# Reordering the first batch of a retention + phase-MLP kernel by the arrival of its loads

## Chip, cores, metric

One core of one Trainium2 chip. The metric is the device time of one execution in microseconds; lower is better. The four times of the kernel before lie between 171.39 and 173.17 us, 1.0% apart, so differences below that rest on several runs taken in turn with the kernel before.

## The reference, cut to what matters

```python
# retention: B=4, H=8, S=768, D=64
state = gamma * state + k_t (outer) v_t ;  x_t = scale * q_t . state
# then, with x of shape (4, 768, 512):
theta = x @ w_theta
zr, zi = x * cos(theta), x * sin(theta)
u = x + w_tok_r @ zr + w_tok_i @ zi       # mixing over the 768 tokens
out = u + max(u @ w_ch, 0)
```

## The kernel before

A **pair** is two 128-row chunks of one batch (three pairs to a batch). For each pair the kernel loads q, k, v in float32, scales and casts them (`prep`), transposes q and k on TensorE (`flip`), forms masked scores (`ret_A`, `ret_mask`), the product with v (`ret_Y`), the part from the state (`ret_I`), the state's update (`ret_S`), theta and its cosine and sine (`theta`), and z (`zmul`). A **tile** is 128 rows of output: `moe_M` (12 mixing matmuls), `moe_u`, `moe_U` (transpose of u), `moe_O`. `w_tok` transposes one block row of the two token weights. The schedule is by hand: in the traces below each engine takes its instructions in the order of the program, so one that waits holds up everything behind it on its engine (2.93 us of TensorE at one place, below). In profile lines PE is TensorE and PEld its loading of weights, DVE is VectorE, ACT ScalarE, POOL GpSimd.

```python
def prep(n, name, engines):                     # cast / scale of a loaded tensor
    ...
        for two in range(2):                    # q and v: one half on each of two engines
            engines[two].tensor_mul(dst[:, two], src[:, two], ...)
def flip(n, name):
    ps = psum.tile([P, 2, NP, P], BF, name="kq_ps", tag="tr", bufs=2)   # two "tr" banks in all
    ... 8 nc.tensor.transpose ...
    nc.vector.tensor_copy(t, ps)
def moe_O(m):
    o_ps = psum.tile([P, dm], FT, name="o_ps", tag="tr", bufs=2)        # the same two banks
    ...
# ---- cut: the first batch, written out call by call ----
for n in range(nG, B * nG + 1):                 # the loop starts at pair 3 (nG = 3)
    ...
    if nxt:
        prep(n + 1, "q", PP)                    # both halves on GpSimd
        prep(n + 1, "v", PP)
    if n == nG:
        w_cast(4)
        nc.gpsimd.tensor_copy(wch, wdma["ch"])
    ...
        theta(n - 1, 0); x_pe(n - 1); theta(n - 1, 1)
    for name, limit in (("k", K_DMA), ("q", Q_DMA)):
        if nxt and n + 1 < limit:
            flip(n + 1, name)                   # in the middle of the iteration
    ...
    ret_S(n, 0); ...; ret_A(n, 1); ret_mask(n, 1); ret_Y(n, 0); ret_I(n, 0)
    moe_U(done)
    moe_M(first, 2, 4)
    if n in (nG, nG + 1):
        w_tok(n - nG + 4)
    moe_M(first, 4, nT)
    moe_u(first)
    ...
    zmul(n - 1, 0); zmul(n - 1, 1)
    for t in done:
        moe_O(t)
        moe_out(t)
```

## Time and profile before

| | before |
|---|---|
| median time | 172.41 us (171.39 to 173.17, 4 runs) |
| span of the profiled run | 170.4 us |
| TensorE (PE) busy | 158.9 us, 93% |
| granted TensorE clock (share of full speed, profiled run) | 1.00 |
| first PE instruction of iterations 4, 5, 6 (`ret_I`, line L241) | 53.25, 63.02, 72.12 us |

The last row is the ruler: iteration n of the loop starts with the state product of the pair before it, so that line's times cut the run into iterations. From iteration 4 on TensorE has no gap; 98.3 us follow the start of iteration 6. The lines themselves are in the prediction.

### The profile page before, as it was taken

What the parts mean: (1) busy time and instruction counts of PE and PEld (TensorE: products, weight loads), DVE (VectorE), ACT (ScalarE), POOL (GpSimd) and SP (SyncE); (2) the same over time, 40 slices, a digit from 0 to 9 for tenths busy, and PEclk for the clock granted to TensorE, in tenths of its full rate; (3) what the DMA queues carried; (4) which work ended last, traced back from release to release, by engine and by line L of the source; (5) the groups of instructions that cost most, each with busy time, mean ns of one, the idle gap of its engine ahead of it and who ended that gap; (6) DMA issues with size and microseconds to landing.
All of it is one profiled execution on the core that took longest, in us unless ns stands there. A gap on an engine that the chain in (4) does not pass through costs nothing.

```text
span 170.4 us, 4701 instructions
## 1 busy us (share of the span) xinstructions
PE 158.9 (93%) x1979; PEld 88.5 (52%) x1979; DVE 101.3 (59%) x139; ACT 82.7 (49%) x141; POOL 62.4 (37%) x81
## 2 busy tenths in 40 slices
PE   7789898988789999999999999999999999999992
PEld 2255465644455766656465645454455444444470
DVE  2457597885657567797486374671755617334443
ACT  8216686770464959677864744828156170000000
POOL 6284839455699588480908163000000000000000
PEclk9999999999999999999999999999999999999999
DMA  4999999999999999999999995976727161464343
GB/s 129 304 341 313 318 302 351 315 377 272 317 304 340 265 295 344 252 210 252 193 286 294 216 260 118 252 96 142 139 51 197 33 175 41 132 192 115 92 154 123
DMA packets 66789, 37.92 MB, mean 223 GB/s; under 512 B 24144, under 2 KB 61264, under 8 KB 66768
## 3 DMA queue, kind: packets, MB, share of 16 engines
q1 hardware_dynamic: 66624, 37.50, 87.2%
q8 instruction: 15, 0.25, 0.6%
q10 hardware_dynamic: 144, 0.13, 0.2%
q14 instruction: 6, 0.05, 0.1%
HBM read 25.69 MB, written 6.29 MB: 188 GB/s over the span
## 4 chain that ended last, share of the span: by engine, by line
PE 77%; DMA 8%; DVE 3%; POOL 3%; ACT 3%; issue 2%; DVEq 0%; POOLq 0%
PE y_ps L328 32%; PE th_ps L302 12%; PE o_ps L356 12%; DMA pair<-in_q_dram 6%; PE at_ps L204 4%; PE kq_ps L183 3%; PE yT_ps L227 3%; PE yT_ps L241 3%; PE st_ps L258 3%; DMA pair<-in_k_dram 2%; PE y_ps L402 2%; DVE at L211 1%; POOL kqb L175 1%; ACT kqb L169 1%; PE w_ps L382 1%
## 5 line engine op out<-in xcount | busy, mean ns | idle before, releaser
L328 PE MATMUL y_ps<-z,wtr 128*128 128x512 bf16 x138 | 52.4, 380 | 1.3 <-DVE u L335 0.8
L328 PE MATMUL y_ps<-z,wti 128*128 128x512 bf16 x138 | 52.3, 379 | 0.0
L335 DVE TENSOR_TENSOR u<-y_ps,x_sb 128x512 bf16<-128x512 f32 x23 | 15.9, 692 | 30.0 <-PE y_ps L328 29.9
L175 POOL TENSOR_TENSOR kqb<-pair,qscp 128x512 bf16<-128x512 f32 x20 | 21.1, 1073 | 33.1 <-DMA pair<-in_q_dram 27.9
L211 DVE TENSOR_TENSOR at<-at_ps,maskp 128x1024 bf16<-128x1024 f32 x24 | 29.3, 1219 | 3.6 <-PE at_ps L204 3.6
L281 ACT CAST xT<-yT_ps 128x512 bf16<-128x512 f32 x22 | 15.0, 738 | 26.3 <-PE yT_ps L227 26.3
L175 POOL TENSOR_TENSOR kqb<-pair,vscp 128x512 bf16<-128x512 f32 x24 | 25.4, 1079 | 4.1 <-DMA pair<-in_v_dram 4.1
L302 PE MATMUL th_ps<-wth,xT 128*128 128x512 bf16 x96 | 23.5, 379 | 0.1
L363 DVE SCALAR_TENSOR_TENSOR ot<-o_ps,u 128x512 f32<-128x512 f32 x23 | 15.8, 689 | 13.0 <-PE o_ps L356 13.0
L356 PE MATMUL o_ps<-wch,uT 128*128 128x512 bf16 x92 | 22.6, 379 | 0.5 <-POOL wch L582 0.5
L328 PEld LDWEIGHTS <-wti 128*128 128x128 bf16 x138 | 13.5, 98 | 14.7 <-issue 1.7
L328 PEld LDWEIGHTS <-wtr 128*128 128x128 bf16 x138 | 13.5, 98 | 13.8
L305 ACT ACTIVATE cs<-th_ps,halfpi 128x512 bf16<-128x512 f32 x24 | 16.5, 688 | 8.3 <-PE th_ps L302 7.9
L272 ACT CAST stbd<-st_ps 64x256 bf16<-64x256 f32 x40 | 14.7, 368 | 11.9 <-PE st_ps L258 11.3
L186 DVE COPY kqT<-kq_ps 128x1024 bf16<-128x1024 bf16 x17 | 11.5, 687 | 11.1 <-PE kq_ps L183 11.1
L312 DVE TENSOR_TENSOR z<-cs,x_sb 128x1024 bf16<-128x1024 bf16 x24 | 17.4, 763 | 0.4 <-DMA x_sb<-xT 0.4
L306 ACT ACTIVATE cs<-th_ps,zerob 128x512 bf16<-128x512 f32 x24 | 16.5, 687 | 0.0
L356 PEld LDWEIGHTS <-uT 128*128 128x128 bf16 x92 | 8.9, 98 | 11.2 <-issue 0.7
L302 PEld LDWEIGHTS <-xT 128*128 128x128 bf16 x96 | 8.9, 98 | 9.9 <-ACT xT L281 0.6
L169 ACT CAST kqb<-pair 128x1024 bf16<-128x1024 f32 x12 | 12.6, 1048 | 1.6 <-DMA pair<-in_k_dram 1.5
L414 ACT COPY uT<-u_ps 128x256 bf16<-128x256 bf16 x2 | 0.7, 373 | 25.5 <-PE u_ps L413 25.5
L183 PE MATMUL kq_ps<-ident,kqb 128*128 128x128 bf16 x136 | 10.1, 219 | 2.9 <-DVE kqb L175 1.0
(57 smaller groups left out, 161.9 us busy)
## 6 DMA issues: line engine op xcount, KB each, us to landing
pair<-in_k_dram SPq DMA_DIRECT2D x12, 512.0 KB, 6.8
pair<-in_q_dram SPq DMA_DIRECT2D x12, 512.0 KB, 7.6
pair<-in_v_dram SPq DMA_DIRECT2D x12, 512.0 KB, 8.0
out_dram<-ot SPq DMA_DIRECT2D x23, 256.0 KB, 2.4
wtok<-in_moe_w_tok_r_dram SPq DMA_DIRECT2D x6, 384.0 KB, 6.8
wtok<-in_moe_w_tok_i_dram SPq DMA_DIRECT2D x6, 384.0 KB, 6.5
w<-in_moe_w_theta_dram SPq DMA_DIRECT2D x1, 1024.0 KB, 8.0
w<-in_moe_w_ch_dram SPq DMA_DIRECT2D x1, 1024.0 KB, 9.2
```

Source lines behind the costliest of these rows:

```text
L175: engines[two].tensor_mul(dst[:, two], src[:, two], _bcast_last(sc[:, 2 * g + two], D))
L183: nc.tensor.transpose(ps[:, two, j, :], st[n, name][:, two, j * P:(j + 1) * P], ident)
L211: nc.vector.tensor_mul(at.rearrange("p a j t -> p (a j) t"), at_ps.rearrange("p a j t -> p (a j) t"), _bcast_mid(maskp[:, two].rearrange(" ...
L281: copy(st[n, "xT"][:, a].rearrange("e j (i w) -> e j w i", w=2), st[n, "y"][a].rearrange("e j (w i) -> e j w i", w=2))
L302: nc.tensor.matmul(th_ps, st[n, "xT"][:, a, j, :], wth[:, j, :], start=(j == 0), stop=(j == NP - 1))
L305: nc.scalar.activation(cs[:, 0, :], th_ps, AF.Sin, bias=halfpi, scale=1.0)
L306: nc.scalar.activation(cs[:, 1, :], th_ps, AF.Sin, bias=zerob, scale=1.0)
L312: nc.vector.tensor_mul(zs[b][:, c], st[n, "cs", a], _bcast_mid(xs[b][:, c, :], 2))
L328: nc.tensor.matmul(y_ps, wT[r][:, s0, t0 * P:(t0 + 1) * P], zs[b][:, s0, r, :], start=(s0 == 0 and r == 0), stop=(s0 == nT - 1 and r == 1))
L335: nc.vector.tensor_add(u, mo[m]["y"], xs[b][:, t0, :])
L356: nc.tensor.matmul(o_ps, mo[m]["uT"][:, j, :], wch[:, j, :], start=(j == 0), stop=(j == nD - 1))
L363: nc.vector.scalar_tensor_tensor(ot, mo[m]["o"], 0.0, mo[m]["u"], ALU.max, ALU.add)
```

## The change

Its intent: put the first batch in an order that fits the times at which the loads land, so that TensorE works where it waited. On GpSimd: k of pairs 2 and 3 is cast there. In PSUM: tile 1 is summed in the state's bank, so tiles 0 and 1 can be open at once. In the loop's iterations 3 to 5 the flips of the next pair go to the end, where their loads have surely landed, with half of q scaled on VectorE.

```diff
-            if m < (B - 1) * nT - 1:
+            if m == 1:
+                y_ps = psum.tile([P, dm], FT, name="y_ps", tag="st", bufs=1)
+            elif m < (B - 1) * nT - 1:
 ... (the first batch's calls in another order; dummy matmuls 31 -> 27) ...
-    prep(2, "k", K)
+    prep(2, "k", (PL,))
-    prep(3, "k", K)
+    prep(3, "k", (PL,))
 ... in the loop:
-        if nxt:
-            prep(n + 1, "q", PP)
-            prep(n + 1, "v", PP)
+        def preps(engines):
+            prep(n + 1, "q", engines)
+            prep(n + 1, "v", PP)
+            if n in (nG, nG + 1):
+                w_cast(n - nG + 4)
         if n == nG:
-            w_cast(4)
             nc.gpsimd.tensor_copy(wch, wdma["ch"])
+        if nxt and n > nG + 2:
+            preps(PP)
+        if n == nG:                      # after ret_A, ret_mask of pair 3
+            moe_u(1)
+            w_tok(2)
         for name, limit in (("k", K_DMA), ("q", Q_DMA)):
-            if nxt and n + 1 < limit:
+            if nxt and nG + 3 < n + 1 < limit:
                 flip(n + 1, name)
+        if n < nG + 3:
+            prep(n + 1, "k", (AC,))      # behind moe_U
-            if n in (nG, nG + 1):
-                w_tok(n - nG + 4)
             moe_M(first, 4, nT)
             moe_u(first)
+            if n < nG + 3:
+                w_tok(n - nG + 3)
 ... zmul(n - 1, 0), zmul(n - 1, 1) ...
-        for t in done:
+        if n < nG + 3:
+            preps(DP)                    # q: one half VectorE, one GpSimd
+        for i, t in enumerate(done):
+            if n < nG + 3:
+                flip(n + 1, "kq"[i])
+                if len(done) == 1:
+                    flip(n + 1, "q")
             moe_O(t)
             moe_out(t)
```

More of the change, by code (lines that the diff above doesn't have):

```diff
@@ L177, in prep, with flip @@
         st[n, name] = t
-    def flip(n, name):
+    def flip(n, name, copy=nc.vector.tensor_copy):
         ps = psum.tile([P, 2, NP, P], BF, name="kq_ps", tag="tr", bufs=2)
@@ L185, in flip, with flip_out @@
         t = work.tile([P, 2, NP, P], BF, name="kqT", bufs=6)
-        nc.vector.tensor_copy(t, ps)
-        st[n, name + "T"] = t
+        if copy:
+            copy(t, ps)
+        st[n, name + "T"], st[n, name + "_ps"] = t, ps
+    def flip_out(n, name):
+        nc.vector.tensor_copy(st[n, name + "T"], st[n, name + "_ps"])
     def flip_dma(n, name):
@@ L288, in x_dma, with x_pe, x_out @@
             in_=st[n, "xT"].rearrange("p a j t -> p (a j t)"))
-    def x_pe(n, lo=0, hi=2):
+    def x_pe(n, copy=nc.vector.tensor_copy):
         b, g = divmod(n, nG)
-        x_ps = psum.tile([P, hi - lo, NP, P], BF, name="x_ps", tag="tr", bufs=2)
-        for a in range(lo, hi):
+        x_ps = psum.tile([P, 2, NP, P], BF, name="x_ps", tag="tr", bufs=2)
+        for a in range(2):
             for j in range(NP):
-                nc.tensor.transpose(x_ps[:, a - lo, j, :], st[n, "xT"][:, a, j, :], ident)
-        nc.vector.tensor_copy(xs[b][:, 2 * g + lo:2 * g + hi, :],
-                              x_ps.rearrange("p a j e -> p a (j e)"))
+                nc.tensor.transpose(x_ps[:, a, j, :], st[n, "xT"][:, a, j, :], ident)
+        st[n, "x_ps"] = x_ps
+        if copy:
+            x_out(n, copy)
+    def x_out(n, copy):
+        b, g = divmod(n, nG)
+        copy(xs[b][:, 2 * g:2 * g + 2, :],
+             st[n, "x_ps"].rearrange("p a j e -> p a (j e)"))
     def theta(n, a):
@@ L376, in w_cast, with w_flip, w_out @@
             wrow[r, t0] = row
+    def w_flip(r, t0, copy=True):
+        w_ps = psum.tile([P, nT, P], BF, name="w_ps", tag="tr", bufs=2)
+        for s0 in range(nT):
+            nc.tensor.transpose(w_ps[:, s0, :],
+                                wrow[r, t0][:, s0 * P:(s0 + 1) * P], ident)
+        wrow[r, t0, "ps"] = w_ps
+        if copy:
+            w_out(r, t0)
+    def w_out(r, t0):
+        (nc.scalar.copy if r else nc.vector.tensor_copy)(
+            wT[r][:, :, t0 * P:(t0 + 1) * P], wrow[r, t0, "ps"])
     def w_tok(t0):
         for r in range(2):
-            w_ps = psum.tile([P, nT, P], BF, name="w_ps", tag="tr", bufs=2)
-            for s0 in range(nT):
-                nc.tensor.transpose(w_ps[:, s0, :],
-                                    wrow[r, t0][:, s0 * P:(s0 + 1) * P], ident)
-            dst = wT[r][:, :, t0 * P:(t0 + 1) * P]
-            if r:
-                nc.scalar.copy(dst, w_ps)
-            else:
-                nc.vector.tensor_copy(dst, w_ps)
+            w_flip(r, t0)
     def moe_last(m):
@@ L447, in keep_busy @@
             nc.tensor.matmul(warm_ps, warm[:, 0:P], warm, start=True, stop=True)
-    DP, PP, K = (nc.vector, nc.gpsimd), (nc.gpsimd, nc.gpsimd), (nc.scalar,)
+    DV, PL, AC = nc.vector, nc.gpsimd, nc.scalar
+    DP, PP = (DV, PL), (PL, PL)
     keep_busy(12)
-    prep(0, "k", K)
-    flip(0, "k")
-    keep_busy(4)
+    prep(0, "k", (AC,))
+    flip(0, "k", None)
     prep(0, "q", DP)
+    flip_out(0, "k")
+    keep_busy(3)
     flip(0, "q")
@@ L464 @@
     state_out(0, 0)
-    keep_busy(1)
     ret_A(0, 1)
     ret_mask(0, 1)
+    ret_Y(0, 0)
+    keep_busy(1)
     ret_S(0, 1)
+    ret_I(0, 1)
     state_out(0, 1)
-    ret_Y(0, 0)
-    ret_I(0, 1)
-    keep_busy(3)
-    prep(1, "k", K)
-    ret_Y(0, 1)
-    ret_out(0, 0, nc.scalar.copy)
-    ret_out(0, 1, nc.vector.tensor_copy)
-    keep_busy(1)
+    prep(1, "k", (AC,))
+    keep_busy(1)
+    ret_Y(0, 1)
+    ret_out(0, 0, DV.tensor_copy)
+    ret_out(0, 1, DV.tensor_copy)
+    keep_busy(3)
+    prep(1, "q", DP)
+    theta(0, 0)
     flip(1, "k")
-    prep(1, "q", DP)
-    x_pe(0, 0, 1)
-    theta(0, 0)
-    x_pe(0, 1, 2)
     theta(0, 1)
     flip(1, "q")
-    keep_busy(2)
     prep(1, "v", PP)
     w_cast(0)
+    x_pe(0, None)
     ret_A(1, 0)
     ret_mask(1, 0)
-    keep_busy(2)
+    x_out(0, DV.tensor_copy)
+    keep_busy(3)
     ret_S(1, 0)
@@ L494 @@
     ret_mask(1, 1)
-    prep(2, "k", K)
     ret_Y(1, 0)
     ret_I(1, 0)
+    w_flip(0, 0)
     ret_S(1, 1)
@@ L500 @@
     ret_I(1, 1)
-    keep_busy(2)
+    ret_Y(1, 1)
+    ret_out(1, 0, AC.copy)
+    ret_out(1, 1, DV.tensor_copy)
+    w_flip(1, 0)
+    prep(2, "k", (PL,))
     zmul(0, 0)
     zmul(0, 1)
-    ret_Y(1, 1)
-    ret_out(1, 0, nc.scalar.copy)
-    w_tok(0)
-    ret_out(1, 1, nc.scalar.copy)
     prep(2, "q", DP)
+    theta(1, 0)
+    theta(1, 1)
     flip(2, "k")
-    theta(1, 0)
+    moe_M(0, 0, 1)
     flip(2, "q")
@@ L514 @@
     w_cast(2)
-    x_pe(1, 0, 1)
-    moe_M(0, 0, 2)
+    x_pe(1, AC.copy)
+    moe_M(0, 1, 2)
     ret_A(2, 0)
     ret_mask(2, 0)
-    theta(1, 1)
-    x_pe(1, 1, 2)
     ret_S(2, 0)
     state_out(2, 0)
+    zmul(1, 0)
     ret_A(2, 1)
@@ L527 @@
     ret_I(2, 1)
-    zmul(1, 0)
+    moe_M(0, 2, 3)
+    ret_Y(2, 1)
+    ret_out(2, 0, AC.copy)
     zmul(1, 1)
-    ret_Y(2, 1)
-    ret_out(2, 0, nc.scalar.copy)
-    ret_out(2, 1, nc.vector.tensor_copy)
+    ret_out(2, 1, DV.tensor_copy)
     w_tok(1)
+    prep(3, "k", (PL,))
+    prep(3, "q", PP)
+    moe_M(0, 3, 4)
     theta(2, 0)
-    x_pe(2, 0, 1)
     theta(2, 1)
-    x_pe(2, 1, 2)
-    moe_M(0, 2, 4)
+    x_pe(2)
+    flip(3, "k", AC.copy)
     zmul(2, 0)
-    prep(3, "k", K)
-    w_tok(2)
-    moe_M(0, 4, 5)
+    moe_M(1, 0, 4)
     zmul(2, 1)
-    flip(3, "k")
-    moe_M(0, 5, nT)
-    moe_u(0)
-    prep(3, "q", DP)
+    flip(3, "q")
     prep(3, "v", PP)
     w_cast(3)
-    moe_M(1, 0, 4)
-    flip(3, "q")
+    moe_M(0, 4, nT)
+    moe_u(0)
     moe_M(1, 4, nT)
-    moe_u(1)
-    w_tok(3)
-    prep(4, "k", K)
     tiles_of = {nG - 2: [], nG - 1: [0, 1]}
@@ L575 @@
             moe_U_dma(done[1])
-        if nxt:
-            prep(n + 1, "q", PP)
+        def preps(engines):
+            prep(n + 1, "q", engines)
             prep(n + 1, "v", PP)
+            if n in (nG, nG + 1):
+                w_cast(n - nG + 4)
         if n == nG:
-            w_cast(4)
             nc.gpsimd.tensor_copy(wch, wdma["ch"])
-        if n == nG + 1:
-            w_cast(5)
+        if nxt and n > nG + 2:
+            preps(PP)
         if late:
@@ L637 @@
                 moe_M(first, 2, 4)
-            if n in (nG, nG + 1):
-                w_tok(n - nG + 4)
             moe_M(first, 4, nT)
             moe_u(first)
+            if n < nG + 3:
+                w_tok(n - nG + 3)
         elif n in pairs:
             moe_M(mine[1], 0, nT)
-        if n + 2 in pairs:
-            prep(n + 2, "k", K)
+        if n + 2 in pairs and n > nG + 1:
+            prep(n + 2, "k", (AC,))
         if late:
```

## The prediction

> Names: a pair is two 128-row chunks of one batch, three pairs to a batch; pair n is worked on by iteration n of the loop, which starts at pair 3. Flip = transpose on TensorE (PE) into the "tr" banks, two in all, each emptied by a copy on VectorE (DVE) or ScalarE (ACT). prep = cast or scaling of a load. T = the end of the last mixing matmul of an iteration's tile. GpSimd is POOL.
>
> **What bounds the kernel now.** I read the slices first, then the chain in order of time, then the timelines of PE and DVE. The slices:
>
> ```profile
> PE   7789898988789999999999999999999999999992
> DMA  4999999999999999999999995976727161464343
> ```
>
> A slice is 4.26 us. PE is full from slice 13 (51 us) on; before that it has gaps, and 31 dummy matmuls (L447) fill others. So only the first 53 us can be shortened; after that, time is PE work. The chain says what held PE there:
>
> ```profile
> 33.74 10.18 DMA pair<-in_q_dram
> 44.06 1.36 POOL kqb L175 x2
> ...
> 48.05 1.59 POOL wrow L375 x2
> 49.64 1.85 POOL wch L582
> 51.53 1.89 PE o_ps L356 x8
> 53.42 0.22 PE yT_ps L241 x4
> ```
>
> q of pair 4 landed at 44.06; PE, in order, had that flip ahead of pair 3's work, and the output products waited for the cast of w_ch, last in POOL's row. Iteration 4 starts at 53.25. PE's timeline of an undisturbed iteration, and DVE's at the same time:
>
> ```profile
> 53.25 0.39 PE L241 MATMUL yT_ps<-kqT,stbd 128*128 128x128 bf16 x4
> ...
> 57.44 1.06 PE L183 MATMUL kq_ps<-ident,kqb 128*128 128x128 bf16 x16
> ...
> 60.62 0.83 PE L382 MATMUL w_ps<-ident,wrow 128*128 128x128 bf16 x12
> ...
> 62.16 1.03 PE L356 MATMUL o_ps<-wch,uT 128*128 128x512 bf16 x4
> 63.02 0.39 PE L241 MATMUL yT_ps<-kqT,stbd 128*128 128x128 bf16 x4
> ```
>
> ```profile
> 62.36 0.69 DVE L335 TENSOR_TENSOR u<-y_ps,x_sb 128x512 bf16<-128x512 f32 x1 [0.64 <-PE y_ps L328]
> 62.97 1.45 DVE L312 TENSOR_TENSOR z<-cs,x_sb 128x1024 bf16<-128x1024 bf16 x2
> 64.34 0.68 DVE L363 SCALAR_TENSOR_TENSOR ot<-o_ps,u 128x512 f32<-128x512 f32 x1
> ```
>
> Flips and w_tok stand in the middle, with mixing matmuls behind them, so PE runs from T = 62.16 into the output product and the next iteration; DVE's u, two z and ot run behind it and nobody waits. Iterations 4, 5, 6 start at 53.25, 63.02, 72.12.
>
> [...] The trace has 1.89 us for a 2048-wide cast (L459) and 0.82 for 768 (L375), so k's 1024 is an estimate of 1.0 to 1.1 us from these, against 1.05 on ACT. [...] In the trace DVE's q half (128x512) takes 0.77 us at 15.83 and 1.17 to 1.22 at 7.39 and 24.05, with POOL busy on its half.
>
> **The change, part by part.** PE's real work is unchanged (four dummies fewer, 0.9 us, in gaps). I lay the new order of each engine by hand along the loads' arrivals seen in before: the start of the POOL instruction that waited for them. PE costs are distances in the dense stretch: flip 0.45, w_tok 0.67, product of four 512-wide matmuls 0.86, full tile 2.59, attention matmuls 0.22 to 0.35 each group; a consumer on DVE sees PE 0.2 us after its last issue.
>
> *Pair 0, 1.* q's DVE half goes ahead of the copy of k, so the first q flip starts at 8.2, not 8.62, and the scores at 9.6, not 10.03. Both xT casts on DVE and theta ahead of the flip: theta starts at about 14.5 (before 15.72), pair 1's scores at 18.0 (18.90). Then v1 and w0 (cast 19.07 to 20.93, bound by the loads) close the gap.
> *Pair 2.* k2 on POOL about 21.9 to 22.95, q2 not before 23.67. Both thetas of pair 1 now precede pair 2's flips; I get pair 2's scores at 26.9 (27.12), its second yT at 30.5 (30.83), the end of its x transposes at 34.0 (34.25), with 0.86 us of tile 0 more done. Ahead by 1.1.
> *Pair 3 and tiles 0, 1.* w2i's cast waits for a row buffer until w_tok(1), to 32.1; k3 on POOL to 33.2; flip at 34.0. Tile 1 in the state's bank need not wait for u of tile 0 (before: a 0.78 us PE gap at 39.08). q3 flips at 36.2, tiles 0 and 1 end at 38.4, the scores of pair 3 at 38.75. w_tok(2), to 39.4. Tile 2 needs its copy, which stands on DVE behind the mask (1.22) and u of tile 1 (0.61): 41.3, a new gap of 1.9. State, scores, yT, u transposes and the rest of tile 2 bring T to **45.2**; before it is at 51.1, with both flips of pair 4 and w_tok 3 and 4 (2.24 us) already done. Net lead 5.9 - 2.24 = **3.7 us**.
>
> *The end of iterations 3, 4, 5.* The flips of the next pair move behind T, and their q half goes to DVE. In DVE's new order stand u, wtr copy, z, z, q half, copy of k, copy of q, ot (iteration 3 has no z and two ot). In iterations 4 and 5, from T: u begins +0.2, wtr copy +0.8, the two z +1.3 (1.37 together), q half +2.65 to +3.75. The q flip cannot start before +3.8. The copy of k follows to +4.4 and frees the bank that the output product needs: +4.4 to +5.26, next iteration. The PE work behind T is 0.67 + 0.45 + 0.45 + 0.86 = 2.43, so PE idles 5.26 - 2.43 = **2.8 us**; 2.4 if the q half runs at 0.77. In iteration 3, without z: q half +1.3 to +2.4, copy of k +3.0, q flip +3.5, ot, second product to +4.5, against 3.29 of work: **1.2 us**.
>
> *Sum.* Iteration 4 starts at 45.2 + 4.5 = 49.7 (before 53.25). From start to T the dense work is 62.16 - 53.25 - 0.67 - 0.9 = 7.3. Iteration 5: 49.7 + 7.3 + 5.26 = 62.2 (63.02). Iteration 6: + 12.5 = 74.7 (72.12). By then the work done is equal. The balance: -3.7 + 1.2 + 2.8 + 2.8 = +3.1 by the terms, +2.6 by the clock, the difference being PE waits of before (about 0.5, at w_ch) that vanish. With 0.3 off for an uncontended q half in iteration 5, about +2.4: 171.76 + 2.4 = **174.2 us**. From iteration 6 the order is as before and PE was dense.
>
> **Rivals.** *A: the intended gain stays.* Without the DVE chain, iteration 3 would end with the flip of q4 at 45.2 and its second output product at 46.5: 6.7 us ahead, less 0.67 for w_tok(4), so 165.7. For it: the loads are there in time (q5 was used at 51.44 with no DMA wait, q6 landed at 59.22, and my iterations need them at 59.6 and 72). Against it: the flips' new place and DVE's order are fixed in the program, and the u that starts the chain cannot run before T. Even a start at 46.5 loses 5.2 to 5.6 in iterations 4 and 5 and ends near 171.
> *B: the loads become the bound.* q4 to q6 leave their buffers later (q6 at 73 instead of 61), so the load seven pair-loads later (v8, issued at 64.96) goes out near 73, and in SP's queue the transpose of k7 (71.28) comes behind it, at about 75, landing 79 (3.8 us to landing); needed near 83. Slack some 4 us. If it is late, 1 to 2 us more: 176.
> *C: contention.* The pair of z took 2.20 at 72.06 with POOL busy, instead of 1.28 to 1.45. Twice that adds 1.5: 175.7. For it: POOL scales q6 and v6 about when iteration 4's z run.
> *D: my front part is too slow.* 150 instructions laid by hand; an error of 1.5 us either way is likely.
>
> **Range and chances.** Centre 174.2. D gives +-1.5, B and C reach up by 1 to 2 each, A bounds the gain near 171. Eight in ten: 171.8 to 176.6. Slower by over 2% is above 175.2, which C or B alone reaches: 0.29. Faster by over 2% is below 168.3, which needs the stalls not to exist: 0.03. Within 2%: 0.68.
>
> **What would show it.** Right: PE gaps ahead of the q flip and of the output product in iterations 4 and 5, 2.4 to 2.9 us in each, released by DVE (q half; copy of k), with no DMA in that chain; iteration 4 starting at 48.5 to 51, 5 at 61 to 63.5, 6 at 73.5 to 76; the wait for q of pair 4 gone; a PE gap near 40 before tile 2's first matmul, released by the wtr copy; PE full from 76 on. Wrong: PE full from iteration 4 on (A); PE waiting for DMA after 50 us (B); iteration 4 starting before 47.5 or after 51.5 (D).

(The casts at L459 and L375 are GpSimd's.)

## The result, and the profile after

The changed kernel takes **181.48 us** (180.42 to 182.78, 4 runs), **5.3% more** (ratio 1.0534, 95% interval 1.0436 to 1.0631). Ratios here are the mean time of one kernel's fast runs over the mean of the other's in the same rounds, so they differ a little from the ratio of the medians. Executions over 1.5% slower than the fastest of the same kernel are left out of the means. The centre of the forecast was slower, 174.2, with 176.6 as the upper end; the size was far more.

The slices of the changed kernel (4.49 us each), against those that the prediction shows of before:

```profile
PE   7989987996798479769999999999999999999992
PEclk9999999999999978978999999999999999999999
DMA  5999999999999937079999999793956135274343
```

TensorE now has holes up to slice 18 (81 us) instead of 51, and behind those of slices 14 and 18 stands a lower granted clock. The DMA engines run dry for a while too (slices 15 and 17, the latter between the two holes), but no wait of TensorE after 50 us is put down to a load. TensorE's timeline, the rows that had idle time in front (in brackets: the idle time and what ended it):

```profile
41.95 0.39 PE L340 MATMUL y_ps<-z,wtr 128*128 128x512 bf16 x1 [1.62 <-DVE wtr L400]
...
56.40 0.41 PE L231 MATMUL yT_ps<-at,kqb 64*64 64x128 bf16 x14 [0.71 <-ACT cs L316]
...
60.34 0.61 PE L183 MATMUL kq_ps<-ident,kqb 128*128 128x128 bf16 x8 [0.58 <-DVE wtr L400]
63.87 0.62 PE L183 MATMUL kq_ps<-ident,kqb 128*128 128x128 bf16 x8 [2.93 <-DVE kqb L175]
...
72.56 0.41 PE L231 MATMUL yT_ps<-at,kqb 64*64 64x128 bf16 x14 [0.71 <-ACT cs L316]
76.50 0.61 PE L183 MATMUL kq_ps<-ident,kqb 128*128 128x128 bf16 x8 [0.58 <-DVE wtr L400]
78.31 0.85 PE L183 MATMUL kq_ps<-ident,kqb 128*128 128x128 bf16 x8 [1.20 <-DVE kqb L175]
```

The front part does what it should: the long wait for q of pair 4 is gone, and iteration 4 starts at 50.69 instead of 53.25. Then iterations 4 and 5 show the same three waits each: on ACT's cosines, on VectorE's copy of the token weights, and on VectorE's half of q. VectorE's own timeline says why the last is so long:

```profile
59.13 0.69 DVE L347 TENSOR_TENSOR u<-y_ps,x_sb 128x512 bf16<-128x512 f32 x1 [2.21 <-PE y_ps L340]
59.73 0.55 DVE L400 COPY wtr<-w_ps 128x768 bf16<-128x768 bf16 x1
60.20 2.17 DVE L322 TENSOR_TENSOR z<-cs,x_sb 128x1024 bf16<-128x1024 bf16 x2
62.29 1.52 DVE L175 TENSOR_TENSOR kqb<-pair,qscp 128x512 bf16<-128x512 f32 x1
63.74 1.49 DVE L187 COPY kqT<-kq_ps 128x1024 bf16<-128x1024 bf16 x2
```

It is busy without a break, and idle for 2.21 us before: u cannot begin until the last mixing matmul, and q's half stands behind u, the copy and two z. And the clock, in the stretches of 1 us around the first hole (columns: window, its length and PE busy, PE weight loads, DVE, ACT, POOL busy, granted clock, DMA share, GB/s):

```profile
64.00:65.00 1.00, 1.00 (x11) 0.66 (x10) 0.89 (x2) 0.00 (x0) 1.00 (x2) 0.94 0.03 10
65.00:66.00 1.00, 1.00 (x6) 0.44 (x5) 0.23 (x2) 0.00 (x0) 1.00 (x2) 0.50 0.29 88
66.00:67.00 1.00, 1.00 (x32) 0.80 (x34) 0.68 (x1) 0.00 (x0) 0.71 (x1) 0.50 0.77 219
67.00:68.00 1.00, 1.00 (x33) 0.80 (x26) 0.99 (x1) 0.58 (x1) 0.00 (x0) 0.50 1.15 384
68.00:69.00 1.00, 1.00 (x5) 0.45 (x4) 0.23 (x1) 0.97 (x4) 0.47 (x1) 0.85 1.04 385
```

TensorE works again from 63.87, but at half speed from about 64.9 to 68.3: (0.06 + 3 x 0.50 + 0.15) / 0.50 = 3.4 us at 0.50. The second hole is followed by the same, 0.77, 0.50, 0.50, 0.52 in the windows from 78 to 82, which is again 3.4 us. The clock record of this trace has both stretches at 0.50 for 3413 ns, and 10.24 us at full speed between them. The prediction has no word of the clock: the profiled run of the kernel before shows 1.00 throughout. (Not all runs of that kernel do: 5 of the 29 taken with the experiments have 0.987 to 0.990. One such stretch would lower the mean by 0.5 x 3.4 / 171 = 0.01, an estimate.)

**Where the 9.1 us of span are** (179.5 against 170.4), by the ruler of iteration starts:

| | before | after | difference |
|---|---|---|---|
| start to iteration 4 | 53.25 | 50.69 | -2.56 |
| iteration 4 | 9.77 | 15.06 | +5.29 |
| iteration 5 | 9.10 | 14.91 | +5.81 |
| iteration 6 to the end | 98.28 | 98.84 | +0.56 |

(One w_tok, 0.67 us of work, moved from before iteration 4 to behind its start, so the front's own gain is 1.9.) Everything lost is in the two iterations.

### The profile page after: what moved, and what is told of

It is laid out like the page before. It is cut to its first block, busy times and chain, and to the rows that moved or that the text cites. A ratio compares the mean times of both kernels' runs of the same rounds, so it can differ in the third digit from the quotient of the medians.

```text
span 179.5 us, 4684 instructions
## 1 busy us (share of the span) xinstructions
PE 162.0 (90%) x1975; PEld 90.7 (51%) x1975; DVE 103.8 (58%) x138; ACT 81.2 (45%) x139; POOL 64.6 (36%) x81
## 4 chain that ended last, share of the span: by engine, by line
PE 74%; DVE 9%; DMA 8%; POOL 2%; issue 2%; ACT 2%; DVEq 0%; SPq 0%; POOLq 0%; ACTq 0%
PE y_ps L340 32%; PE o_ps L368 11%; PE th_ps L312 10%; DMA pair<-in_q_dram 8%; PE at_ps L208 4%; PE yT_ps L231 3%; PE st_ps L262 3%; PE kq_ps L183 3%; PE yT_ps L245 3%; POOL kqb L175 2%; DVE at L215 2%; DVE z L322 2%; DVE kqb L175 2%; PE y_ps L419 1%; DVE wtr L400 1%
## 5 line engine op out<-in xcount | busy, mean ns | idle before, releaser
L175 POOL TENSOR_TENSOR kqb<-pair,qscp 128x512 bf16<-128x512 f32 x18 | 20.3, 1141 | 35.4 <-DMA pair<-in_q_dram 13.7
L285 ACT CAST xT<-yT_ps 128x512 bf16<-128x512 f32 x20 | 13.5, 736 | 38.5 <-PE yT_ps L231 38.4
L175 POOL TENSOR_TENSOR kqb<-pair,vscp 128x512 bf16<-128x512 f32 x24 | 25.9, 1098 | 4.9 <-DMA pair<-in_v_dram 3.9
L368 PE MATMUL o_ps<-wch,uT 128*128 128x512 bf16 x92 | 24.1, 396 | 0.0
L375 DVE SCALAR_TENSOR_TENSOR ot<-o_ps,u 128x512 f32<-128x512 f32 x23 | 15.8, 690 | 14.0 <-PE o_ps L368 14.0
L340 PEld LDWEIGHTS <-wtr 128*128 128x128 bf16 x138 | 13.5, 98 | 15.8 <-DVE wtr L400 1.8
L276 ACT CAST stbd<-st_ps 64x256 bf16<-64x256 f32 x40 | 14.7, 367 | 13.5 <-PE st_ps L262 12.9
L340 PEld LDWEIGHTS <-wti 128*128 128x128 bf16 x138 | 13.5, 98 | 13.2
L183 PE MATMUL kq_ps<-ident,kqb 128*128 128x128 bf16 x136 | 11.2, 225 | 6.8 <-DVE kqb L175 4.1
L183 PEld LDWEIGHTS <-kqb 128*128 128x128 bf16 x136 | 9.2, 101 | 11.0 <-DVE kqb L175 5.4
L208 PE MATMUL at_ps<-kqT 64*64 64x128 bf16 x384 | 11.0, 228 | 2.4 <-DVE at L215 1.8
L387 POOL CAST wrow<-wtok 128x768 bf16<-128x768 f32 x12 | 10.6, 900 | 5.8 <-PE w_ps L393 5.2
```

What stands on the lines that cost most here:

```text
L175: engines[two].tensor_mul(dst[:, two], src[:, two], _bcast_last(sc[:, 2 * g + two], D))
L183: nc.tensor.transpose(ps[:, two, j, :], st[n, name][:, two, j * P:(j + 1) * P], ident)
L208: nc.tensor.matmul(at_ps[half, par, j, :], kT[rows, two, j, half], qT[rows, :, j, half], start=(j == 0), stop=(j == NP - 1), skip_group_ch ...
L340: nc.tensor.matmul(y_ps, wT[r][:, s0, t0 * P:(t0 + 1) * P], zs[b][:, s0, r, :], start=(s0 == 0 and r == 0), stop=(s0 == nT - 1 and r == 1))
L368: nc.tensor.matmul(o_ps, mo[m]["uT"][:, j, :], wch[:, j, :], start=(j == 0), stop=(j == nD - 1))
L375: nc.vector.scalar_tensor_tensor(ot, mo[m]["o"], 0.0, mo[m]["u"], ALU.max, ALU.add)
```

## The experiments

All outputs are right. Theory **S**: the flips' late place, with VectorE's order behind the last mixing matmul, makes the holes, and the holes make the half clock. Rivals: the front's order or the casts on GpSimd cost the time; the holes are waits for loads; the clock is a side effect.

### The flips back in the middle

```diff
-        if nxt and n > nG + 2:
+        if nxt:
             preps(PP)
-            if nxt and nG + 3 < n + 1 < limit:
+            if nxt and n + 1 < limit:
-        if n < nG + 3:
-            prep(n + 1, "k", (AC,))
-        if n + 2 in pairs and n > nG + 1:
+        if n + 2 in pairs:
... and preps(DP) and the flips at the end removed; prep(4, "k") at the end of the front
```

> The changed kernel with its new front part, but in iterations 3 to 5 the flips of the next pair stand in the middle of the iteration again, q is scaled on GpSimd alone, and k's cast goes back to where it was. Theory (the late flips, with q's half behind the two z on VectorE, make the loss): iteration 3 waits for q of pair 4 as before, to about 46.9 us, iteration 4 starts near 52.3, iterations 4 and 5 take 9.8 each, no TensorE gap over 0.5 us and full clock after 53 us: 172 us, give or take 0.7. Rival (the new front order or the k casts on GpSimd cost the time): stays above 177.

Measured: **174.04 us** (ratio to before 1.0127, interval 1.0058 to 1.0197; clock 0.999). 7.4 of the 9 us are gone, so the rival that the front's order costs the time falls. It is 2 us above what I expected. Its TensorE timeline shows what is left:

```profile
44.05 0.39 PE L340 MATMUL y_ps<-z,wti 128*128 128x512 bf16 x1 [3.75 <-ACT wti L400]
...
62.27 1.02 PE L368 MATMUL o_ps<-wch,uT 128*128 128x512 bf16 x4 [0.58 <-DVE wtr L400]
```

The second wait stands in iterations 3, 4 and 5 (0.57, 0.58, 0.57), 1.7 us together: w_tok is still behind the last mixing matmul, and the output product takes a "tr" bank that the copy has to empty first. The first is of my edit's making: k's cast of pair 4, which waits for its load, stood ahead of the copy on ACT. Iteration 4 started at 52.63 all the same. And these 3.75 us, the longest hole shown here, were not followed by half clock in this trace: length alone does not decide it (see "What stays open").

### Dummy matmuls in the hole

```diff
                 if len(done) == 1:
+                    for _ in range({nG + 1: 12, nG + 2: 5}[n]):
+                        nc.tensor.matmul(warm_again, warm[:, 0:P], warm, start=True, stop=True)
                     flip(n + 1, "q")
```

> The changed kernel with 12 dummy matmuls (2.6 us) in iteration 4 and 5 (1.1 us) in iteration 5 put between the k flip and the q flip, where TensorE sits idle. They shorten no wait. Theory (a third of the loss is the clock, which the trace shows at 0.50 for some 3.4 us after each of the two long gaps): granted clock 1.00 throughout, iteration 5 starts 0.4 us earlier and itself takes 1.1 less, and so on: 178.3 us. Rival (the clock is a side effect and costs nothing): 181.5, unchanged.

Measured: **178.43 us** (ratio 1.0374, interval 1.0312 to 1.0435), clock 1.000, 0.999, 1.000, 0.997 in its four runs, where the changed kernel has 0.981, 0.972, 0.987, 0.972. That is the 178.3 expected: work that is of no use makes the kernel **3.0 us faster**, so the half clock is a third of the loss. Twice 3.4 us at half speed would cost at most 3.4 us of work, an estimate from the windows of the profiled run, which fits (by their clock, the two runs at 0.972 had about three such stretches: 0.028 x 180 / (0.5 x 3.4) = 3.0, also an estimate).

### The two z behind the output sums

```diff
-        if late:
+        if late and n >= nG + 3:
             zmul(n - 1, 0)
             zmul(n - 1, 1)
...
             moe_O(t)
             moe_out(t)
+        if late and n < nG + 3:
+            zmul(n - 1, 0)
+            zmul(n - 1, 1)
```

> The changed kernel with the two z products of iterations 4 and 5 moved on VectorE behind the output sums, so that q's half and both copies follow the wtr copy at once. Theory (the chain u, wtr, z, z, q half, copy of k on VectorE sets the end of iterations 4 and 5): from the last mixing matmul to the next iteration 4.0 us instead of 6.8 and 5.6, longest TensorE gap about 1.2 us, no clock drop: 175.4 us. Rival (the gap is TensorE waiting for q's load or for GpSimd's half): the q flip still starts at 63.9 and 78.3, 181 us.

Measured: **175.49 us** (ratio 1.0194, interval 1.0132 to 1.0257), clock 0.998. No instruction was removed and no buffer added; four multiplications moved on VectorE, and 6.0 us went; some 3 of them, by the run with the dummies, are the clock, which is full again. The holes in its TensorE timeline, iteration 4:

```profile
56.20 0.41 PE L231 MATMUL yT_ps<-at,kqb 64*64 64x128 bf16 x14 [0.70 <-ACT cs L316]
60.13 1.26 PE L183 MATMUL kq_ps<-ident,kqb 128*128 128x128 bf16 x16 [0.57 <-DVE wtr L400]
```

The two flips are one row now, stretched to 1.26, and the 2.93 us are gone. So the hole was VectorE's order, not q's load. The waits on the cosines and on the copy remain.

### q on GpSimd alone, flips still late

```diff
         if n < nG + 3:
-            preps(DP)
+            preps(PP)
```

> The changed kernel with q of pairs 4 to 6 scaled by GpSimd alone (both halves), flips still late. Theory (VectorE chain): the q flip no longer waits, the output product still waits for the copy of k behind the two z; 4.2 us from the last mixing matmul to the next iteration, 0.5 to 1 us more where the z contend with GpSimd; no clock drop: 175.8 us. Rival (what counts is q's scaling wherever it is done): GpSimd's second half comes later by 1.0 to 1.5 us and the gap stays near 3 us: 181.

Measured: **177.08 us** (ratio 1.0294, interval 1.0221 to 1.0366). The q flip no longer waits, and as expected the wait has moved one step on, to the output product, whose bank needs the copy of k that stands behind the two z:

```profile
60.12 1.05 PE L183 MATMUL kq_ps<-ident,kqb 128*128 128x128 bf16 x16 [0.58 <-DVE wtr L400]
62.80 1.02 PE L368 MATMUL o_ps<-wch,uT 128*128 128x512 bf16 x4 [1.63 <-DVE kqT L187]
```

Two of its four runs have a clock of 0.988 and 0.989, and take 178.06 and 177.51; the two at 0.998 and 1.000 take 176.16 and 176.65. The hole of 1.63 us above is from the run with 176.16, at 0.998; the holes of the other three were not profiled.

### The late flips alone, on the kernel before

```diff
 (kernel before, its own front part)
+        if nxt and n > nG + 2:
+            preps(PP)
+            nc.gpsimd.tensor_copy(wch, wdma["ch"])
             w_cast(4)
-            nc.gpsimd.tensor_copy(wch, wdma["ch"])
-            if nxt and n + 1 < limit:
+            if nxt and nG + 3 < n + 1 < limit:
... and preps(DP) with the flips at the end, as in the change
```

> The kernel before with its own front part, and only the loop's change: in iterations 3 to 5 the flips of the next pair at the end, q's half on VectorE behind the two z (and w_ch cast ahead of the w4 rows). Theory (the loss is the late flips with VectorE's order): gaps of 2.5 to 4 us ahead of the q flip and the output product in iterations 4 and 5, the 0.7 us wait for the ACT cosines, the clock at 0.50 for some 3.4 us after a long gap: iterations 4 and 5 take 13.5 to 15 us each, 182 us, give or take 2. Rival (the loss needs the new front part): under 175.

Measured: **183.68 us** (ratio 1.0683, interval 1.0631 to 1.0734), clocks 0.969 to 0.988. Iterations 4 and 5 take 13.5 and 14.3 us (starts at 54.39, 67.86, 82.14). The loss needs nothing of the new front part. Holes of 2.14 us ahead of the q flip, with no w_tok beside them, were followed by half clock: 0.50 in the windows from 68 to 70 us.

### Single parts on the kernel before

```diff
 (tile 1)
+            if m == 1:
+                y_ps = psum.tile([P, dm], FT, name="y_ps", tag="st", bufs=1)
```

> The kernel before with one part: tile 1 summed in the state's bank. It removes the 0.78 us TensorE gap that ended with u of tile 0, at 39. Theory: TensorE waits for q of pair 4 until 44 afterwards all the same, so the gain is swallowed there: ratio 0.997 to 1.003. Rival: the 0.8 us stay, ratio 0.995.

Measured: 173.10 us, ratio **1.005** (interval 1.0002 to 1.0098). Rather a loss than a gain, and neither theory's number. In its profile the gap at u of tile 0 is gone, and TensorE waits longer for q of pair 4 afterwards:

```profile
45.66 0.40 PE L183 MATMUL kq_ps<-ident,kqb 128*128 128x128 bf16 x4 [0.99 <-POOL kqb L175]
46.66 0.40 PE L183 MATMUL kq_ps<-ident,kqb 128*128 128x128 bf16 x4 [0.60 <-POOL kqb L175]
```

Its six runs fall in two groups: clock 1.000, 0.989, 1.000 with 172.60, 172.53, 171.96 us, and 0.98 with 173.59, 174.46, 174.76 us (the last is left out of the ratio). The first group equals before: the gain is swallowed, as expected. That the second lost its time to half clock after the longer wait is not shown: only the clock beside each time speaks for it, and the profiled run was of the first group.

```diff
 (k on GpSimd)
-    prep(2, "k", K)
+    prep(2, "k", (nc.gpsimd,))
-    prep(3, "k", K)
+    prep(3, "k", (nc.gpsimd,))
```

> The kernel before with one part: k of pairs 2 and 3 cast on GpSimd. Estimate from the changed kernel's rows: 1.04 us each, the same as on ACT, and TensorE waits for q of pair 4 later in any case: ratio 0.997 to 1.003. Rival: GpSimd's row becomes the bound in the front, q of pair 2 or 3 come 1 us later and the kernel loses 0.5 us or more: ratio over 1.003.

Measured: 171.86 us, ratio **0.9973** (interval 0.9937 to 1.0008): no difference that the runs can tell, as expected.

### The bank wait on the cosines

In before, the flips stood between theta and the first yT product. That product takes the banks of theta's sums, which ACT empties by its cosine and sine; with the flips gone it comes 0.9 us earlier and has to wait.

```diff
-        if not two and n + 1 >= K_DMA:
+        if not two:
             moe_M(first, 2, 4)           # now between theta and yT in iterations 3 to 5
...
-            if n + 1 < K_DMA:
-                moe_M(first, 2, 4)
```

> The changed kernel with two of tile n's mixing steps (0.86 us) moved from behind the u transposes to behind theta in iterations 3 to 5, so that they stand between theta and the first yT product, where the flips stood before. Theory (the 0.71 us TensorE waits on the ACT cosines are a bank wait that the flips used to cover): both waits vanish, the chain from the last mixing matmul on is unchanged: 180.1 us, 1.4 less than the changed kernel's 181.5. Rival (the time is given back at the q flip, which waits for VectorE): 181.5.

Measured: **178.47 us** (ratio 1.0397, interval 1.0335 to 1.0459). Both waits on the cosines are gone from its timeline, so their cause is shown. The gain is 3.0 by the medians, not 1.4: the two z of iteration 4 take 1.32 instead of 2.17 and q's half 0.68 instead of 1.52, so the hole shrinks too (in the changed kernel GpSimd is busy beside them, from 59.55 to 66.7; that it meets them less here was not shown), and in the profiled run the half clock behind it is gone:

```profile
61.37 0.62 PE L183 MATMUL kq_ps<-ident,kqb 128*128 128x128 bf16 x8 [1.23 <-DVE kqb L175]
```

One half-clock stretch is then left in the profiled run, around the start of iteration 6 (clock 0.990), behind a hole of 1.20 us.

### A version that beats both

From the changed kernel: late flips in iteration 3 alone, where q of pair 4 lands late; in iterations 4 and 5 in the middle with q on GpSimd; w_tok between the mixing matmuls, where its copies delay nobody; w_tok(2) between tiles 0 and 1.

```diff
-        if nxt and n > nG + 2:
+        if nxt and n > nG:
             preps(PP)
-            if nxt and nG + 3 < n + 1 < limit:
+            if nxt and nG + 1 < n + 1 < limit:
-        if n < nG + 3:
+        if n == nG:                      # three times: late k cast, late preps, late flips
+            if n < nG + 3:
+                w_tok(n - nG + 3)
             moe_M(first, 4, nT)
             moe_u(first)
-            if n < nG + 3:
-                w_tok(n - nG + 3)
-            moe_u(1)
-            w_tok(2)
+            moe_u(1)
     moe_M(0, 4, nT)
     moe_u(0)
+    w_tok(2)
     moe_M(1, 4, nT)
... and prep(n + 2, "k") at the end of every iteration, as in before
```

> The changed kernel with what the runs so far point to: late flips only in iteration 3 (where q of pair 4 lands late), in iterations 4 and 5 in the middle with q on GpSimd; w_tok between the mixing matmuls instead of behind them; w_tok(2) between tiles 0 and 1 so that its copy goes ahead of the mask. Theory: iteration 4 starts at 48.5 to 49.5, 9.8 us for each of iterations 4 and 5, iteration 6 at 68 to 69 against 72.1 before: 168.3 us, ratio 0.98. Rival (the loads become the bound once TensorE is ahead): a TensorE wait for q of pair 6 at about 62, 170.5 us.

Measured: **169.87 us** (169.28 to 170.43, 6 runs), ratio to before **0.9868** (interval 0.9835 to 0.9901), clock 1.00 within 0.002. That is 1.3% faster: the interval lies below 1, and it is 1.6 us more than expected. Iterations 4 and 5 take 9.8 us each and start at 49.83 and 59.59; iteration 6 at 69.36. No wait for q of pair 6, so the rival falls. Two holes are left in iteration 3:

```profile
42.06 0.38 PE L262 MATMUL st_ps<-kqb 64*64 64x64 bf16 x12 [0.96 <-DVE u L347]
48.37 0.61 PE L183 MATMUL kq_ps<-ident,kqb 128*128 128x128 bf16 x8 [1.08 <-DVE kqT L187]
```

The first is the price of the state's bank for tile 1: pair 3's state cannot start before u of tile 1 has emptied it, and u stands behind the mask. A last version puts u of tile 1 ahead of that mask, q's half ahead of the token copy, and u of tile 2 behind the output sums.

```diff
+        if n == nG:
+            moe_u(1)
         if n in pairs:
             ret_A(n, 0)
             ret_mask(n, 0)
-        if n == nG:
-            moe_u(1)
 ... (cut: further down, behind moe_M(first, 2, 4)) ...
+            if n == nG:
+                preps(DP)                # ahead of w_tok(3)
... moe_u(first) of iteration 3 moved behind moe_out
```

> The run before (late flips in iteration 3 only), with VectorE's order in iteration 3 mended: u of tile 1 ahead of the mask, q's half of pair 4 ahead of the wtr copy, u of tile 2 behind the output sums. Theory (the two gaps that its trace shows in iteration 3, 0.96 us on u and 1.08 us on the copy of k, are VectorE's order): the first shrinks to about 0.4, the second to about 0.45, iteration 4 starts near 48.7 instead of 49.8: 168.8 us, ratio 0.98. Rival (q of pair 4, landing at 44, holds VectorE and with it the wtr copy): no gain, 169.9.

Measured: 169.74 us, ratio 0.9862 (interval 0.9813 to 0.9911). The same as the version before it, and not the 168.8 expected. Iteration 4 does start at 48.39, 1.4 us earlier, but iteration 6 at 69.08, 0.3 earlier: 0.33 us are given back on u of tile 2 and 0.50 on VectorE in iteration 5, where the two z take 2.97 us instead of 2.35. That VectorE would be the next limit is likely from this, but was not tested.

## Why the prediction was wrong, by its own steps

- **The bound, and the direction**: right. Only the time before 53 us could be shortened; from iteration 6 on both kernels take the same 98 to 99 us.
- **The front part**: right within its margin. Iteration 4 at 49.7 said, 50.69 measured; tile 2's gap of 1.9 said, 1.62 measured, released by the wtr copy as said.
- **"The end of iterations 3, 4, 5"**: right in mechanism, off in its sizes. TensorE idled 0.58 + 2.93 = 3.5 us there in iteration 4 and 0.58 + 1.20 = 1.8 in iteration 5, where 2.8 twice was said: the sum is near by luck, one over and one under. The 0.58 ahead of the k flip was not forecast; the gap ahead of the output product, on the copy of k, was forecast and did not come. From the last mixing matmul to the next iteration, 5.26 us were said; 58.93 to 65.75 is 6.8, and 75.09 to 80.66 is 5.6. The terms that were off: the two z with GpSimd beside them (1.37 said, 2.09 from start to start in iteration 4) and q's half (1.1 said, 1.45), which is rival C in the first of the two and the opposite in the second (1.20 and 0.61); and the clock.
- **"From start to T the dense work is ... 7.3"**: this step failed. It was taken from the iteration before, flips subtracted. But the flips were also the cover for ACT's emptying of theta's banks; taken away, they leave a wait of 0.71 us, twice, and start to T takes 8.2 us in iteration 4, not 7.3. I subtracted work and did not ask what it had been hiding. The run with mixing steps in that place removed both waits.
- **"PE idles 2.8 us" as the whole cost of a hole**: this step failed, and it is the largest. A hole was priced at its own length, with TensorE at full speed afterwards. It cost 3.4 us at half clock as well, in both iterations: 3.0 us of the 9, shown by the dummies. With that, iteration 5 starts at 65.75 instead of 62.2 and iteration 6 at 80.66 instead of 74.7. When the holes were made short (the z moved), iterations 4, 5, 6 started at 50.49, 62.38 and 74.28. Counted from differences of the starts, the 5.9 us by which iteration 6 came late are about: the front 1.0, the cosines' wait 0.9 twice, z and q's half +1.1 and -0.6, and the half clock 2.4; another 0.6 of it falls behind that start, 3.0 in all, as with the dummies.
- **Rivals**: A (no stalls) did not come; with the flips back in the middle in iterations 4 and 5 the best version reaches 169.9, where A said 165.7. B (loads) did not occur: in no profiled run was a TensorE wait after 50 us put down to a load. C came in iteration 4.
- **The range**: it let C and B add 1 to 2 us each, but it had no term for what a hole costs beyond its length. An upper end of 176.6 could not hold 181.5.
- **Two sums**: with the q half at 0.77 the idle time is 2.8 - 0.33 = 2.5, not 2.4, and +2.6 less 0.3 is 2.3, not 2.4. Neither matters here.

What stays open: how long a hole TensorE can stand. Holes of 1.2 to 2.9 us, with transposes around them, were followed by half clock in the profiles; the version with a hole of 1.63 us in its profile had a lower clock in two of its four runs (0.988, 0.989). But in one run, with the mixing steps moved, a hole of 1.23 us left the clock at 1.00 and one of 1.20 did not, and 3.75 us with the flips in the middle did not lower it either. The traces say a little more. In the 3.413 us just before each of five half-speed stretches (these 3.413 us begin at 61.47 and 75.13 in the changed kernel, 63.72 and 77.37 with the late flips alone, 70.71 with the mixing steps moved) TensorE is busy for 0.30 to 0.48 of the time, and for 0.03 to 0.14 if transposes are left out. But the hole of 3.75 us, from 40.30 to 44.05, has no matmul at all for longer than that, and no half clock came behind it. So neither the length of a hole nor how little TensorE does in 3.4 us explains all of these traces by itself. What decides was not shown: no run tested it, and these shares come from five stretches and modelled matmul ends.

## What to carry to other kernels

Price a hole on TensorE twice: its own length, and the half-speed stretch that may follow (here 3.4 us at 0.50 behind holes of 2.93 and 1.20 us); and where a hole can't be removed, fill it with dummy matmuls, which here bought 3.0 us. Before work is moved away from a place, ask what it was covering there (here, the emptying of two banks), and what stands ahead of its inputs in the in-order queue of the engine that makes them: four multiplications moved behind it on VectorE were worth 6.0 us. A late place makes sense where the load is late: the best version uses it there and nowhere else. (That it pays in iteration 3 was not tested by itself.)
